# Batch 1's first product: four f tiles dense, eight as seven block products

## The chip, the cores and the metric

The kernel runs on one core of a Trainium2 chip. The metric is the device time of one execution in microseconds. TensorE (PE) multiplies, VectorE (DVE), ScalarE (ACT) and GpSimd (POOL) work on elements, and SyncE (SP) issues the transfers.

## The reference

An attention with two softmaxes gives a token matrix x, and a gated network follows it. Shapes: q, k, v are 8 x 8 x 576 x 64 (batch, head, token, width), p is 8 x 8 x 32 x 64, w_a and w_b are 512 x 1536, w_out is 1536 x 512.

```python
def _attn_ref(q, k, v, p):
    scale = 1.0 / np.sqrt(q.shape[-1])
    def sm_attn(qq, kk, vv):
        s = scale * np.matmul(qq, kk.transpose(0, 1, 3, 2))
        s = s - np.max(s, axis=-1, keepdims=True)
        a = np.exp(s)
        a = a / (np.sum(a, axis=-1, keepdims=True) + 1e-09)
        return np.matmul(a, vv)
    p_packed = sm_attn(p, k, v)
    return sm_attn(q, p_packed, p_packed)
...
x = np.ascontiguousarray(attn_out.transpose(0, 2, 1, 3)).reshape(B * S, H * D)
a = x @ w_a
b = x @ w_b
out = a * b @ w_out
```

## The kernel before, in words

The token matrix is never formed. For each batch the second softmax's weights (256 rows, head and packed token, by 576 tokens, called a2) are kept, and the packed values (ppT) are multiplied with w_a and w_b first: that gives g, 256 rows by 2 x 1536 columns. The first product is then a2 with g, twelve f tiles of 128 columns each for a and b; h is their product; the second product is h with w_out. float32 accuracy comes from splitting each operand in a high and a low part (`_hi`, `_lo`) and three passes: high with high, high with low, low with high. The low part is a subtraction, `lo_part`, on the engine that is named in its call (VectorE, if none is).

**Dense form** (`mm1`, `mm1_half`, L406 to L435; batches 0 and 1). An f tile is 24 matmuls of 288 columns: two halves (a, b) by two halves of the tokens by two row blocks by three passes. The g tiles come from `g_tiles` (L382), with the weights `w_ab` in SBUF, as pairs or single f tiles.

**Block form** (`period`, `product`, L790 to L909; batches 2 to 7). The product of a 2 x 2 block matrix is taken with seven products instead of eight, of sums and differences of the blocks. One f tile is 7 x 3 = 21 matmuls of 288 columns. The sums of the weights come from `make_g` (L801, for two f tiles at once: matmuls, three copies on ScalarE, two sums and a low part on VectorE, a low part and a difference on GpSimd) and `split_g` (G_hi on ScalarE, G_lo on GpSimd, step name "G"); those of a2 from `half_sum` and `half_parts` (steps t0 to t3 and u0 to u3). `split_h` (step "H") makes h_hi on ScalarE and h_lo on GpSimd. Products 1, 5, 3 and 6 go to bank pair X, products 2, 4 and 7 to V; `c` and `d` hold partial sums of them. A period n ends f tile n and begins n + 1: products 5, then 1 and 2 of the next tile; copy X to d on ScalarE; matmuls of the second product as filling; d = V + d on VectorE; products 3, then 6 of the next; c and one multiplication; filling; products 4, then 7 of the next; addition of c and one multiplication; filling. The numbers of filling matmuls stand in `FILLS`.

The weights arrive as float64 words and are converted in batch 0 in three steps, A (high word, ScalarE), B (low word, on the engine that `WAYS` names: 0 ScalarE, 1 VectorE, 2 GpSimd) and C (both joined, VectorE); D splits w_out. `w_ab` is written to DRAM once (`w_kept`, six parts of 1 MB), and `make_g` reads a part for every two f tiles (`load_kept`, tile `wr`).

Every engine works in order. The order is written out by hand: `PLAN_0`, `PLAN` and `STEPS` name the steps between two half f tiles or in the places of a period. `S`, `r` are steps of the first softmax of the next batch, `s` of the second, `k`, `q` transposes of loaded tiles, `L..` loads, `P`, `T` turns of the packed tokens. In batch 1 the dense first product comes first, then a block of 96 matmuls of the second product (`mm2_third`), then two periods (-2 and -1) that begin batch 2's first f tile, then the loop. Three parts of `w_kept` are written after batch 0's second product has been issued in large part, three more at the fourth step of batch 1.

Of the kernel before, what the change touches and what calls it, by code (L numbers as in the profile page):

```python
# [19 lines left out]
def tile_packed_attn_gated_ffn(  # L20
# [20 lines left out]
    nc = tc.nc  # L41
# [14 lines left out]
    NB = 2  # L56
# [15 lines left out]
    scratch = early.__enter__()  # L72
    plain = tc.tile_pool(name="plain", bufs=1, side="right")
# [8 lines left out]
    w_ab = plain_p.tile([P, NC, R, 4 * P], F32, name="w_ab")  # L82
# [39 lines left out]
    def turn(key, b, i):  # L122
# [4 lines left out]
        xTs.setdefault((b, key), []).append(xT)  # L127
# [207 lines left out]
    def stage2(b, e):  # L335
# [43 lines left out]
    ghi = plain_p.tile([P, E, 4, 2 * P], F32R, name="ghi")  # L379
    glo = plain_p.tile([P, E, 4, 2 * P], F32R, name="glo")  # L380

    def g_tiles(b, *groups, s=False):  # L382

        for fts in groups:
# [7 lines left out]
            for r in range(R):  # L392
                for e in range(E):
                    rows = slice(64 * e, 64 * e + 64)
                    w = w_ab[rows, c, r, :].rearrange("p (a u f) -> p u a f", a=2, u=2)
# [23 lines left out]
    def mm1(b, ft, between):  # L419
# [11 lines left out]
        hh = h_hi[ft][:, c0:c0 + S]  # L431
        flat = asb.rearrange("p u t -> p (u t)")
        nc.scalar.copy(out=hh, in_=flat)
        lo_part(h_lo[ft][:, c0:c0 + S], flat, hh, nc.vector if b == 0 and HLO[ft] == "1" else nc.gpsimd)
# [35 lines left out]
    def out_tile(i):  # L470

        if i % 3 == 1:
            return sm.tile([P, DO], F32, name="wo_f32", bufs=1)
# [12 lines left out]
    def emit(b, plan, tasks={}):  # L486

        for name in plan.split():
            if name in tasks:
                next(tasks[name], None)  # L490
                continue
# [30 lines left out]
            elif what == "Lp":  # L522
# [5 lines left out]
    START = ("Y7 k1 X4 k0 T0 k2 k3 k4 q1 B S0 r0 r1 S1 q0 r1 r0 q2 r0 r1 q4 r0 r1 q3 A P0 A X3 Lp2 A s0 s1 s0 "  # L528
             "s1 C Z8 s1 X3 s0 B A B Z9 C B X7 A B C C X5 X15 C s0 A s1 B s0 s1 A B Lk2 B B A s0 B s1 s1 C s0 "
             "s1 g A")  # L530
    WAYS = ("200000020222122211202100021202110111")
    TURN = ("1000100010")
# [3 lines left out]
    PLAN = (" |  |  | S0 | r0 | r0 |  | r0 |  | r0 Lv1 ; S1 | r1 | r1 q0 Lk2 | r1 | r1 | q1 Lk3 Lv2 P0 |  ; s0 | s0 s0 | s0 T2 | "  # L536
            "s0 Lp4 | s0 s1 | s1 s1 | s1 | s1 | s1 | t0 t1 t2 t3 u0 | k2 |  | k3 Lq2")
    PLAN = dict(enumerate(PLAN.split("|")))
    PLAN_0 = ("Lk1 A A B C B C B A C | C B C | A A B | B C A A C A C | | B Lp2 C Lv0 B | | | C k0 T0 B | A A C "
# [447 lines left out]
```

## Time and profile before

| what | value |
|---|---|
| median of 3 runs | 708.11 us (707.4 to 709.52) |
| profiled execution, span from first to last instruction | 705.6 us |
| TensorE busy | 699.4 us (99%) |
| VectorE, ScalarE, GpSimd busy | 455.9, 356.9, 417.1 us |
| instructions | 14386 |

The profiled execution's own time is known by its span; the median of the runs is 2.5 us above it, which holds what lies around the span. A row of a stretch gives the busy time of each engine in it, with the number of instructions in brackets. In the chain a row gives where a piece begins, how long it lasts, and what it is, with the number of instructions; pieces in which TensorE runs one matmul after the other give the spacing of matmuls, while the mean duration of a single matmul holds its way through the array as well. Of a group of instructions the busy time and the mean ns of one are given, then the idle time ahead of them and what ended it.

### The profile page before, as it was taken

To read this page: it belongs to the slowest core of one execution; us is meant where nothing else is said; L and a number is where in the kernel's file an instruction comes from. 1 tells how busy PE (TensorE), PEld (TensorE's weight loads), DVE (VectorE), ACT (ScalarE), POOL (GpSimd) and SP (SyncE) were. 2 spreads that over 40 slices of the span, in tenths; PEclk is the share of its full clock that TensorE was granted. 3 is DMA by queue.
4 is the path that set the end of the run, shared out by engine and by line. 5 is a ranking of instruction groups with operands and counts; after the bars stand their busy time and mean duration, and the time that the engine had idled before them with its cause. 6 is when DMAs were issued, how large, how long until landed. Compare 5 with 4: busy or idle time off the path is not lost.

```text
span 705.6 us, 14386 instructions
## 1 busy us (share of the span) xinstructions
PE 699.4 (99%) x5654; PEld 582.8 (83%) x5654; DVE 455.9 (65%) x833; ACT 356.9 (51%) x719; POOL 417.1 (59%) x321
## 2 busy tenths in 40 slices
PE   9999999999999999999999999999999999999998
PEld 7888878898788888878888788888888878888886
DVE  4997765467365679566775678765785667754332
ACT  3778724554244555535554455554545446544520
POOL 1596741337254777646863589566775578856520
PEclk9999999999999999999999999999999999999999
DMA  9999986753254736356434664556145323133002
GB/s 316 380 229 297 282 233 136 252 106 93 69 141 161 170 89 172 115 139 168 119 95 124 173 161 95 131 165 173 63 123 154 106 91 119 60 124 117 1 1 75
DMA packets 179460, 102.65 MB, mean 145 GB/s; under 512 B 145728, under 2 KB 161344, under 8 KB 174016
## 3 DMA queue, kind: packets, MB, share of 16 engines
q1 hardware_dynamic: 179392, 101.73, 50.7%
q8 instruction: 44, 0.72, 0.4%
q14 instruction: 24, 0.20, 0.1%
HBM read 85.98 MB, written 15.73 MB: 144 GB/s over the span
## 4 chain that ended last, share of the span: by engine, by line
PE 91%; DVE 4%; issue 1%; DMA 1%; ACT 1%; SPq 1%; DVEq 0%
PE x L754 36%; PE m L796 28%; PE m L414 11%; PE m L440 5%; PE x L810 4%; PE s L326 2%; PE s L341 1%; PE x L396 1%; PE s L280 1%; DMA qn<-in_q_dram 1%; PE s L316 1%; DVE a_lo L93 1%; DVE part L764 0%; DVE d L878 0%; DVE w_ab L212 0%
## 5 line engine op out<-in xcount | busy, mean ns | idle before, releaser
L754 PE MATMUL x<-wo,h_hi 128*128 128x512 f32 (+1 forms) x776 | 249.4, 391 | 0.0
L93 POOL TENSOR_TENSOR h_lo<-asb,h_hi 128x576 fp32r<-128x576 f32 x95 | 139.0, 1465 | 76.0 <-ACT h_hi L841 42.8
L754 PEld LDWEIGHTS x<-wo,h_hi 128*128 128x128 f32 x776 | 140.8, 188 | 22.1 <-ACT part L762 0.8
L754 PE MATMUL x<-wo,h_lo 128*128 128x512 f32 (+1 forms) x388 | 152.2, 392 | 0.0
L93 POOL TENSOR_TENSOR G_lo<-gs,G_hi 128x640 fp32r<-128x640 f32 x72 | 113.1, 1577 | 29.6 <-ACT G_hi L831 29.4
L754 PEld LDWEIGHTS x<-wo,h_lo 128*128 128x128 f32 x388 | 72.9, 188 | 11.7
L93 POOL TENSOR_TENSOR A_lo<-gs,A_hi 128x256 fp32r<-128x256 f32 x36 | 27.2, 755 | 89.3 <-ACT A_hi L819 89.3
L878 DVE TENSOR_TENSOR d<-m,d 128x576 f32<-128x576 f32 (+1 forms) x73 | 54.1, 741 | 34.7 <-ACT d L874 33.9
L891 DVE TENSOR_TENSOR asb<-m,d 128x288 f32<-128x288 f32 x72 | 32.5, 451 | 63.2 <-ACT c L887 59.9
L887 ACT COPY c<-m 128x288 f32<-128x288 f32 x72 | 28.8, 400 | 82.5 <-PE m L796 82.5
L764 DVE TENSOR_TENSOR part<-x,part 128x512 f32<-128x512 f32 (+1 forms) x65 | 44.1, 678 | 38.8 <-PE x L754 38.8
L796 PE MATMUL m<-tx_hi,G_hi 128*128 128x288 f32 x216 | 63.8, 296 | 0.0
L796 PE MATMUL m<-tx_hi,G_lo 128*128 128x288 f32 x216 | 63.6, 295 | 0.0
L796 PE MATMUL m<-tx_lo,G_hi 128*128 128x288 f32 x216 | 63.2, 293 | 0.0
L816 ACT COPY gs<-x 128x512 f32<-128x512 f32 x35 | 20.6, 588 | 82.2 <-PE x L810 80.6
L831 ACT CAST G_hi<-gs 128x640 fp32r<-128x640 f32 x72 | 52.2, 729 | 15.7 <-POOL gs L825 15.1
L874 ACT COPY d<-m 128x576 f32<-128x576 f32 (+1 forms) x73 | 46.7, 640 | 19.2 <-PE m L796 18.8
L841 ACT CAST h_hi<-asb 128x576 fp32r<-128x576 f32 x72 | 49.0, 680 | 11.5 <-DVE asb L905 11.5
L796 PEld LDWEIGHTS m<-a_hi,G_hi 128*128 128x128 f32 x144 | 27.0, 187 | 31.9 <-issue 17.4
L825 POOL TENSOR_TENSOR gs<-gs 128x512 f32<-128x512 f32 x36 | 46.7, 1297 | 3.2 <-DVE gs L822 2.9
L796 PE MATMUL m<-a_hi,G_hi 128*128 128x288 f32 x144 | 46.6, 324 | 0.0
L904 DVE TENSOR_TENSOR m<-m,c 128x288 f32<-128x288 f32 x72 | 33.3, 463 | 17.0 <-PE m L796 15.3
(189 smaller groups left out, 1568.9 us busy)
## 6 DMA issues: line engine op xcount, KB each, us to landing
wr<-w_kept SPq DMA_DIRECT2D x36, 1024.0 KB, 5.1
nat<-in_k_dram SPq DMA_DIRECT2D x56, 144.0 KB, 4.7
nat<-in_q_dram SPq DMA_DIRECT2D x56, 144.0 KB, 5.3
vt<-in_v_dram SPq DMA_DIRECT2D x28, 256.0 KB, 3.9
out_dram<-part SPq DMA_DIRECT2D x27, 256.0 KB, 2.1
raw<-in_moe_w_a_dram SPq DMA_DIRECT2D x12, 512.0 KB, 8.7
raw<-in_moe_w_b_dram SPq DMA_DIRECT2D x12, 512.0 KB, 8.7
raw<-in_moe_w_out_dram SPq DMA_DIRECT2D x12, 512.0 KB, 6.9
```

What stands on the lines that cost most here:

```text
L93: return eng.tensor_tensor(out=dst, in0=src, in1=hi.bitcast(F32), op=ALU.subtract)
L414: nc.tensor.matmul(out=ps[:, half, 0:HS], lhsT=gt[:, kt, ft % 4, cols], rhs=at[:, kt, HS * half:HS * half + HS], start=(n == 0 and kt == 0 ...
L440: nc.tensor.matmul(out=o[:, cols], lhsT=ht[:, c0:c0 + P], rhs=wt[:, cols], start=(ft == 0 and n == 0), stop=(ft == NFT - 1 and n == 2))
L754: nc.tensor.matmul(out=o[:, cols], lhsT=ht[:, c0:c0 + P], rhs=wt[:, cols], start=(ft == fts[0] and n == 0), stop=end)
L764: nc.vector.tensor_tensor(out=parts[i][:, cols], in0=o[:, cols], in1=parts[i][:, cols], op=ALU.add)
L796: nc.tensor.matmul(out=bank[:, n % 2, 0:HS], lhsT=g, rhs=t, start=(first and i == 0), stop=(i == 2), skip_group_check=True)
L825: nc.gpsimd.tensor_tensor(out=gs[:, 2:4].rearrange("p a u f -> p a (u f)"), in0=gs[:, 0:2].rearrange("p a u f -> p a (u f)"), in1=s2.unsqu ...
L831: nc.scalar.copy(out=G_hi[:, n % 3], in_=gs[:, 1:6, n % 2])
L841: nc.scalar.copy(out=view(h_hi[ft]), in_=src)
L874: nc.scalar.copy(out=d[:, both], in_=X[:, both, 0:HS])
L878: nc.vector.tensor_tensor(out=d[:, both], in0=V[:, both, 0:HS], in1=d[:, both], op=ALU.add)
L904: nc.vector.tensor_tensor(out=v, in0=v, in1=c2, op=ALU.add)
```

## The change

Batch 1 keeps the dense form for f tiles 0 to 3 and takes the block form for f tiles 4 to 11 (`NB` 1, `F0` 4). Its second product, a block before, now fills the periods 3 to 11, first the first third of all five token tiles (60 matmuls), then the second third of three (36). The two periods ahead of batch 2 and the block of 96 matmuls go. Batch 1's a2 is kept in two layouts: split in full for the dense tiles, then with its differences (steps h0 to h3, j1 to j3) for the block form. Batch 2's attention moves to the steps of batch 1's new plan (`PLAN_1`, `STEPS_1`). Of periods 4 to 11's low parts, five of h and two of G are made by VectorE (`HLO_1`, `GLO`), the others by GpSimd. The six parts of `w_kept` are all written within batch 0 (`K0`, `K1` in the plan, then 5, 4, 3, 2), and the part for f tiles 4 and 5 is loaded ahead of batch 0's last output tile. Tiles take over space of others: `wr` and `gs` that of the weights' parts 0 and 1, `parts` and `d` that of the dense g tiles, `tf` and `A` share one place. `WAYS` and `PLAN_0` get a new order; the plan ahead of batch 0's first product (`START`) stays.

```diff
-    NB = 2
+    NB = 1
+    F0 = 4
...
-    w_ab = plain_p.tile([P, NC, R, 4 * P], F32, name="w_ab")
+    w_ab = [kp.tile([P, R, 4 * P], F32, name=f"w_ab{c}", tag=("wr", "gs")[c]) for c in range(2)]
+    w_ab += [plain_p.tile([P, R, 4 * P], F32, name=f"w_ab{c}") for c in range(2, NC)]
...
-            yield
-            return
-        hi, lo = (t[:, e, :].rearrange("p (x u l) -> p u x l", u=2, l=TL) for t in (a2_hi, a2_lo))
+            if b > NB:
+                yield
+                return
+        rows = "p (u x l) -> p u x l" if halves else "p (x u l) -> p u x l"
+        hi, lo = (t[:, e, :].rearrange(rows, u=2, l=TL) for t in (a2_hi, a2_lo))
...
-    WAYS = ("200000020222122211202100021202110111")
+    WAYS = "200200200222112212222102021211120001"
...
+    for _ in pieces:
+        emit(0, "A B C D")
+    for c in (5, 4, 3, 2):
+        keep_weights(c)
+    for i, c0 in enumerate(tiles):
+        if i == len(tiles) - 1:
+            while slot[0] <= max(PLAN_0):
+                between()
+            g_tiles(1, (0, 1), (2,), s=True)
+            load_kept(F0)
...
-        lo_part(G_lo[:, n % 3], gs[:, 1:6, n % 2], G_hi[:, n % 3], nc.gpsimd)
+        lo_part(G_lo[:, n % 3], gs[:, 1:6, n % 2], G_hi[:, n % 3], nc.vector if GLO[n:n + 1] == "1" else nc.gpsimd)
...
-            lo_part(view(h_lo[ft]), src, view(h_hi[ft]), nc.gpsimd)
+            lo_part(view(h_lo[ft]), src, view(h_hi[ft]), nc.vector if HLO_1[n:n + 1] == "1" else nc.gpsimd)
...
+    GLO, HLO_1 = "010000010100", "010111010101"
+    FIRST_FILLS = ((6, 1, 5), (5, 0, 2), (4, 1, 0), (5, 5, 2), (4, 8, 0), (6, 4, 2), (3, 9, 0), (10, 0, 4), (4, 6, 0))
+    STEPS_1 = {3: {'pre': 'r0', 'a': 'j2 G', 'w': 'r0', 'end': 'S1 Lv1'}, 4: {'pre': 'r1', 'd': 'H', 'v': 'Lk2 r1', 'h': 'q0', 'f': 'r1 r1 G'}, 5: {'d': 'q1 r1', 'a': 'H', 'c': 'P0', 'f': 'G', 'end': 'Lv2'}, 6: {'post': 's0 Lp4 T2', 'v': 's0', 'b': 'G', 'f': 'H s0'}, 7: {'post': 's0', 'a': 'H', 'h': 's0', 'b': 's0 G', 'w': 'Lk3', 'f': 's1'}, 8: {'pre': 's1', 'v': 's1', 'c': 's1 H', 'f': 's0 G'}, 9: {'pre': 'G', 'd': 's1 H k2', 'h': 's1', 'w': 's1 t0', 'end': 't1'}, 10: {'d': 'H', 'v': 'u0 t2', 'a': 'G t3', 'end': 'u1'}, 11: {'v': 'k3', 'a': 'H Lq2', 'w': 'u2 G', 'f': 'u3'}}
+    PLAN_1 = ("h0 h1 h2 j1 h3 | e S0 | j3 | Lq1 M r0 | r0 | | r0 E | Lq0")
...
+    for ft in range(F0):
+        mm1(1, ft, between)
...
+    filler[0] = first_parts()
+    for n in range(F0 - 1, LAST):
```

In `PLAN_1` the name e is the single g group for f tile 3, M is `make_g(4)` and E is `split_g(4)`; h and j are `half_sum` and `half_parts` for batch 1.

## Rows read from the trace of the kernel before

**Rows 1.** The page: span, and busy time of TensorE.

```profile
span 705.6 us, 14386 instructions
...
PE 699.4 (99%) x5654; PEld 582.8 (83%) x5654; DVE 455.9 (65%) x833; ACT 356.9 (51%) x719; POOL 417.1 (59%) x321
```

**Rows 2.** Stretches: PE, PEld, DVE, ACT, POOL busy, granted clock, DMA share, GB/s.

```profile
31.20:80.60 49.40, 49.31 (x469) 42.57 (x469) 41.48 (x67) 38.73 (x71) 38.88 (x24) 1.00 0.97 292
...
118.30:191.90 73.60, 73.60 (x673) 63.16 (x679) 39.08 (x62) 33.43 (x66) 30.48 (x24) 1.00 0.53 135
191.90:358.00 166.10, 166.03 (x1331) 137.33 (x1332) 113.89 (x214) 86.04 (x181) 110.60 (x87) 1.00 0.51 136
```

**Rows 3.** Waits of TensorE: us in total, times, longest.

```profile
PE m L414 <- ACT ghi L402: 0.9, 1, 0.9
```

**Rows 4.** The chain that ended last: start, us, what.

```profile
125.35 0.61 PE m L396 x16
125.96 0.86 PE x L396 x16
...
133.96 3.20 PE m L414 x24
...
167.12 5.46 PE x L754 x24
172.58 1.02 PE m L810 x16
...
193.74 1.40 PE m L796 x9
...
199.52 1.20 PE m L796 x9
```

**Rows 5.** Groups of batch 1's stretch on TensorE, shapes apart.

```profile
L414 PE MATMUL m<-a_hi,ghi 128*128 128x288 f32 x96 | 21.4, 304 | 0.0
```

**Rows 6.** Groups of VectorE, shapes apart: busy us, mean ns, idle before.

```profile
L878 DVE TENSOR_TENSOR d<-m,d 128x576 f32<-128x576 f32 x71 | 53.2, 749 | 30.3 <-ACT d L874 29.5
L764 DVE TENSOR_TENSOR part<-x,part 128x512 f32<-128x512 f32 x63 | 43.2, 686 | 37.0 <-PE x L754 37.0
...
L904 DVE TENSOR_TENSOR m<-m,c 128x288 f32<-128x288 f32 x72 | 33.3, 463 | 17.0 <-PE m L796 15.3
L905 DVE TENSOR_TENSOR asb<-m,d 128x288 f32<-128x288 f32 x72 | 33.0, 458 | 2.5
L891 DVE TENSOR_TENSOR asb<-m,d 128x288 f32<-128x288 f32 x72 | 32.5, 451 | 63.2 <-ACT c L887 59.9 <-POOL G_lo L93 1.4 <-POOL h_lo L93 0.7
L93 DVE TENSOR_TENSOR a_lo<-t,a_hi 128x288 fp32r<-128x288 f32 x24 | 20.1, 857 | 0.6 <-ACT a_hi L646 0.6
...
L821 DVE TENSOR_TENSOR gs<-x,gs 128x256 f32<-128x256 f32 x35 | 14.8, 424 | 22.9 <-ACT A_hi L818 21.3 <-ACT A_hi L819 1.4
...
L93 DVE TENSOR_TENSOR A_lo<-x,A_hi 128x256 fp32r<-128x256 f32 x35 | 14.6, 418 | 0.0
...
L93 DVE TENSOR_TENSOR tx_lo<-tf,tx_hi 128x576 fp32r<-128x576 f32 x6 | 11.9, 1983 | 1.1 <-POOL h_lo L93 1.1
...
L286 DVE TENSOR_REDUCE nmx<-s 128x1 f32<-128x576 f32 x15 | 11.2, 749 | 0.4 <-PE s L280 0.4
```

**Rows 7.** Groups of GpSimd, shapes apart.

```profile
L93 POOL TENSOR_TENSOR h_lo<-asb,h_hi 128x576 fp32r<-128x576 f32 x95 | 139.0, 1465 | 76.0 <-ACT h_hi L841 42.8 <-ACT h_hi L433 32.3
L93 POOL TENSOR_TENSOR G_lo<-gs,G_hi 128x640 fp32r<-128x640 f32 x72 | 113.1, 1577 | 29.6 <-ACT G_hi L831 29.4
```

**Rows 8.** Line 93 alone: duration ns min/median/max, first and last start.

```profile
L93 DVE TENSOR_TENSOR h_lo<-asb,h_hi x1: 759/759/759, 69.0 to 69.0; 128x576 fp32r<-128x576 f32 x1
```

**Rows 9.** Transfers by line: count, KB each, median us to landing.

```profile
wr<-w_kept SPq DMA_DIRECT2D x36, 1024.0 KB, 5.1
...
w_kept<-w_ab SPq DMA_DIRECT2D x6, 1024.0 KB, 7.1
```

**Rows 10.** SP in order of time, 80 to 120 us.

```profile
97.54 2.24 SPq L626 DMA_DIRECT2D w_kept<-w_ab  x3
...
116.00 1.77 SPq L467 DMA_DIRECT2D out_dram<-asb  x4
```

More of the change, by code (lines that the diff above doesn't have):

```diff
@@ L430, in mm1 @@
         c0 = 64 * (b % 2)
[L431 to L434, printed above, removed]
+        hh, hl, src = h_hi[ft][:, c0:c0 + S], h_lo[ft][:, c0:c0 + S], asb.rearrange("p u t -> p (u t)")
+        if b:
+            hh, hl = (t.rearrange("p (x u l) -> p u x l", u=2, l=TL) for t in (hh, hl))
+            src = asb.rearrange("p u (x l) -> p u x l", l=TL)
+        nc.scalar.copy(out=hh, in_=src)
+        lo_part(hl, src, hh, nc.vector if b == 0 and HLO[ft] == "1" else nc.gpsimd)
         between()
@@ new lines, in tile_packed_attn_gated_ffn, with between, load_kept @@
+    slot = [0]
+    def between():
+        emit_steps(1, PLAN_0.get(slot[0], ""))
+        slot[0] += 1
+    for ft in range(NFT):
+        if ft % 2 and ft + 1 < NFT:
+            g_tiles(0, (ft + 1, ft + 2))
+        mm1(0, ft, between)
+    LAST = NFT * (B - NB)
+    wr_of, A_of, parts = {}, [], []
+    def load_kept(n):
+        if n < LAST:
+            t = kp.tile([P, R, 4 * P], F32, name="wr", tag="wr")
+            nc.sync.dma_start(out=t.rearrange("p r f -> p (r f)"), in_=w_kept[n // 2 % NC])
+            wr_of[n] = t
@@ new lines, in tile_packed_attn_gated_ffn @@
+    tiles = tiles_of(0)
+    pairs = [bank_pair() for _ in range(2)]
+    banks = [pairs[i % 2][:, i // 2, :] for i in range(4)]
+    for f in range(9):
+        for i, c0 in enumerate(tiles):
+            mm2_part(banks[i], c0, [f])
+        between()
[3 more added lines that the diff above has]
+        keep_weights(c)
+    for i, c0 in enumerate(tiles):
+        if i == len(tiles) - 1:
+            while slot[0] <= max(PLAN_0):
+                between()
+            g_tiles(1, (0, 1), (2,), s=True)
+            load_kept(F0)
+        for f in range(9, NFT, 3):
+            mm2_part(banks[i], c0, range(f, f + 3))
+            between()
+        mm2_out(0, banks[i], c0, i)
@@ L747, in flush, with mm2_steps @@
             pend.pop(0)()
-    def mm2_steps(o, c0, fts, then, cols=slice(0, DO)):
+    def mm2_steps(o, c0, fts, then, cols=slice(0, DO), first=True, last=True):
         for ft in fts:
@@ L754, in mm2_steps @@
                 nc.tensor.matmul(
-                    out=o[:, cols], lhsT=ht[:, c0:c0 + P], rhs=wt[:, cols], start=(ft == fts[0] and n == 0), stop=end)
-                if end:
+                    out=o[:, cols], lhsT=ht[:, c0:c0 + P], rhs=wt[:, cols],
+                    start=(first and ft == fts[0] and n == 0), stop=(last and end))
+                if end and then:
                     pend.append(then)
@@ L872, in period @@
         if here or there:
[L873 removed]
+            d = d_of[n] = late["d"][:, n % 2]
             nc.scalar.copy(out=d[:, both], in_=X[:, both, 0:HS])
@@ new lines, in tile_packed_attn_gated_ffn @@
+    for ft in range(F0):
+        mm1(1, ft, between)
+    while slot[0] <= max(PLAN_1):
+        between()
+    t = kp.tile([P, 4, DO], F32, name="parts", tag="ghi")
+    parts += [t[:, i] for i in range(4)] + [late["part"]]
+    t = kp.tile([P, 4 * DO], F32, name="tf_d", tag="glo")
+    late["tf"] = t[:, 0:3 * HS].rearrange("p (i c) -> p i c", i=3)
+    late["d"] = t[:, 3 * HS:7 * HS].rearrange("p (i u c) -> p i u c", i=2, u=2)
+    banks_of["x"], banks_of["v"] = bank_pair(), bank_pair()
+    paired[0] = True
```

176 lines of the change are left out of this document (61 added, 115 removed), and 4 rows, old and new, of the table PLAN_0.

## The prediction

> **What bounds the kernel now.** I read the page's first part, then the stretches, then TensorE's waits, then the chain that ended last. TensorE is busy for 699.4 of 705.6 us [rows 1]. A busy TensorE is not yet one at its peak, so the stretches come next: in batch 0's first product (31 to 81 us), in batch 1's stretch (118.3 to 191.9 us) and in two batches' worth of the loop (191.9 to 358 us) TensorE is busy nearly throughout at the full granted clock, while VectorE, ScalarE and GpSimd are each busy for less [rows 2]. After the start TensorE's own row of waits has one entry, 0.9 us [rows 3]. The chain stays on TensorE, and its spacing can be read there: 24 dense matmuls of 288 columns take 3.20 us, nine block matmuls of the same width 1.20 us, both 0.133 us each; 24 matmuls of 512 columns take 5.46 us, 0.2275 us each [rows 4]. So TensorE runs at its own rate. Time falls by what its list of matmuls loses and rises by any wait that comes in.
>
> **The change part by part.**
>
> *The products.* A dense f tile is 24 matmuls; batch 1's 288 are three groups of 96, of which one row is shown [rows 5]. The change leaves 4 x 24 dense ones and makes 8 tiles of seven products with three passes each, 8 x 21 = 168. Removed: 192 x 0.133 = 25.6 us. Added: 168 x 0.133 = 22.4 us. Difference: -3.2 us.
>
> *Forming g.* Removed are two of the three single groups (0.61 us each) and three pairs (0.86 us each): 3.8 us. Added are four block formings at n = 4, 6, 8 and 10, at the 1.02 us of the one at 172.58 us: 4.1 us [rows 4]. Difference: +0.3 us. The single group for f tile 3 and the forming for batch 2 stay.
>
> *Second product.* The first third of batch 1 (5 tiles) and three tiles of the second third are 8 x 12 = 96 matmuls of 512 columns in both kernels; they now stand between the block products. Difference: 0.
>
> *Going to and fro.* After a group of narrow matmuls the first wide ones are late: nine block matmuls behind a forming take 1.40 us, elsewhere 1.20 [rows 4], so 0.2 us a change. Batch 1's stretch has some nine such places and the new one, with its formings apart from the attention groups, one or two more; bounds 0 and +0.5, taken as +0.1.
>
> TensorE's list therefore gets shorter by 2.8 us. Whether anything stands idle for it is the rest.
>
> *VectorE in the new stretch.* Batch 1's stretch of 73.6 us [rows 2] less 288 x 0.133, 96 x 0.2275, three singles and three pairs, one forming and the twelve block matmuls ahead of batch 2 leaves 6.3 us for attention and changes. From f tile 4 on the new stretch holds nine periods: 180 matmuls at 0.133 (24.0), 96 at 0.2275 (21.8), four formings (4.1) and nearly all of those 6.3 us, say 5.8: 55.7 us of TensorE. VectorE's work I take from the loop: 113.89 us for two batches [rows 2], 57 us per batch of twelve periods. The new stretch lacks four of twelve periods' own operations (0.749 + 0.451 + 0.463 + 0.458 = 2.12 us each, 8.5), two of six formings (0.424 twice and 0.418, 2.5), six of nine additions to parts (0.686 each, 4.1) and half of the first softmax, by estimate two operations of 0.749, 1.5 [rows 6]. That leaves 40.4, and 41.3 with one more split at 0.857 [rows 6]. To it come the differences that now go to VectorE instead of GpSimd: five of h and two of G. The one h difference that VectorE made in this trace took 0.759 us [rows 8]; by size (640 instead of 576 elements) one of G is 0.84. The seven cost 5.5 us. But the same subtraction at the same size, tx_lo, averages 1.983 us [rows 6]; at this price the seven cost 5 x 1.98 + 2 x 2.2 = 14.3. So VectorE has 46.8 to 55.6 us to do in 55.7 us, 84 to 100%, where the loop stands at 69% [rows 2]. On average it fits at either end.
>
> A queue that is so full answers late. Behind a late difference on VectorE stand the addition into d (0.749), the two multiplications for h and the addition of c; the third and fourth product, and the next period's second product, wait for the banks that these read. In the written order an even period ends with 2 to 4 matmuls of the second product and an odd one is followed by a forming, so that about 0.5 to 1 us of lateness is covered; without that cover each lateness is TensorE's. The worst places are period 5 (a transpose of q ahead of the addition into d, and only five filling matmuls), period 9 (a softmax transpose, which waits for GpSimd's multiplication, ahead of the addition of c) and periods 10 and 11 (the splits of batch 2's transposed weights). Bounds: 0, and 7 x (1.983 - 0.759) = 8.6 us if every one of the seven is slow and all of it reaches TensorE. I take +0.4, near the lower end, because GpSimd loses the same seven operations (five of 1.465, two of 1.577 us [rows 7]) and with them work that VectorE could collide with.
>
> The tx_lo row against the h row shows a VectorE subtraction that takes 2.6 times as long in one place as in another. The Trainium skill ("SBUF — State Buffer", section "SBUF: two separate sides") states that a VectorE instruction with two SBUF inputs and a GpSimd instruction exclude one another from a shared port pair, and that whoever starts second is blocked for the other's whole length. The two rows agree with it so far. By that rule most of the seven would stand near tx_lo's figure, and the sum would be the third case below.
>
> *Writing and reading w_kept.* The same six writes of 1 MB, but parts 0 and 1 go out within the second product of batch 0 and 5, 4, 3, 2 behind them. A write takes 7.1 us to land [rows 9]; the three of before are issued from 97.54 us [rows 10], 20 us ahead of batch 1, so four have time even at twice that. SP then passes the stores of three output tiles, the last of which ends at 117.8 us [rows 10], and issues the load of part 2 there; it lands 5.1 us later [rows 9], near 123. The first forming stands behind four half tiles (6.4 us), the group for f tile 3 (0.6) and a scores group (0.6), near 126 us. Cover of 3 us; at the 7.1 us of a write 1 us of it is left, and without it the forming and all that TensorE has behind it wait, by 1 or 2 us at most. I take 0. Later loads have two periods, some 12 us, for their 5.1.
>
> *New places in SBUF.* tf, x5, d, parts, gs and A take over space of weights, g tiles and an output tile. Their first writers wait for the last readers: GpSimd's half sums for the writes of parts 4 and 5, which are out first; the first d and parts for dense f tile 3, which TensorE has then just finished. V's bank waits for VectorE's product of tile 3 (0.75 us and a hand-over), behind three matmuls (0.4 us) and the transposes of a softmax that the step ahead issues. Bounds 0 and 0.5; it is within the 0.4 above.
>
> *Batch 0's new order.* Of the 36 low-word conversions GpSimd now makes 16 instead of 13, ScalarE 11 instead of 13, VectorE 9 instead of 10. GpSimd is busy 38.9 of 49.4 us there [rows 2] and can take more, but the h differences behind come later, and with them the buffer that ScalarE's next copy needs. TensorE's list is unchanged, so that little can be won. Bounds -0.3 and +1.5; taken as 0.
>
> Sum: 705.6 - 3.2 + 0.3 + 0.1 + 0.4 = 703.2 us of span. The median of the runs is 708.11, 2.5 us above the span of the profiled execution, and I leave that as it is: **705.7 us**.
>
> **The rivals.**
> (1) *The gain comes, as above.* TensorE's list is surely shorter, and the loop runs the same block products at their full rate beside a busy VectorE. 704.3 to 706.0. Chance 0.51.
> (2) *VectorE's queue eats it.* TensorE waits some 0.35 us at each of the seven, about 2.5 us: 708.1 - 2.8 + 2.5 = 707.8. A late load (1 to 2 us) or GpSimd's conversions (up to 1.5) lead to the same case. For it: 84 to 100% against 69. Against: the loop too has periods that take the splits of the transposed weights, and no wait of TensorE shows there [rows 3]. 706.0 to 710.2. Chance 0.34.
> (3) *Slower, by one mechanism:* the seven differences each get tx_lo's 1.983 us, ahead of what TensorE wants, and the lateness can't be made up, since VectorE idles in other places of the period. Of the 8.6 us two thirds reach TensorE, 5.7: 708.1 - 2.8 + 5.7 = 711.0. It decides from 4.9 us on. For it: the tx_lo row. Against: less GpSimd work to collide with. 710.2 to 713. Chance 0.15.
>
> **How the numbers follow.** 0.3% (2.1 us) is about what a measurement of this kernel can't tell from no change: faster is below 706.0, slower above 710.2. Faster 0.51, same 0.34, slower 0.15. The low end of the range is the whole list with nothing lost and the small change of batch 0 won, with about half a microsecond of spread, 704.3; the high end cuts into the third case, 709.9. The likeliest case's own range is 704.3 to 706.0.
>
> **What the next profile would show.** Dense matmuls: 384 instead of 576; block matmuls 1680 instead of 1512. From batch 1's first matmul to the first step of batch 2's own periods: 70.8 to 71.5 us instead of 73.6, at 0.133 us a matmul, with no gap over 0.4 us. Wrong, if the h differences on VectorE average over 1.5 us and the gaps behind the addition into d add up to over 1 us; if the load of part 2 lands behind 126 us; if batch 1 starts later than 118.6 us; or if two batches of the loop behind it no longer take the time they took.

## The result and the profile after

The changed kernel takes 712.26 us (median of five runs, 711.95 to 712.98) where the kernel before took 708.09 beside it: a ratio of 1.0053, interval 1.0041 to 1.0066. It is about 4 us slower; 2.4 us less had been forecast. In every run of this case the time lies 1.73 to 1.86 us above the span. So the profile of the kernel before, of 705.6 us, belongs to a run of 707.4, the quickest of its five; of the 2.5 us between that span and the median 0.7 come from this, and only 1.8 lie around the span. The profile below is of a run of 712.11. The two spans differ by 4.7 us, the medians by 4.2.

The page of the changed kernel first, span and busy times, as [rows 1]:

```profile
span 710.3 us, 14408 instructions
...
PE 701.7 (99%) x5614; PEld 580.3 (82%) x5614; DVE 472.1 (66%) x870; ACT 365.8 (51%) x742; POOL 439.6 (62%) x337
```

TensorE is busy 2.3 us longer although its list of matmuls got shorter, which says that a busy TensorE can be a slow one. So the stretches come next, as [rows 2]: batch 0's first product, 73.6 us from batch 1's start, and two batches of the loop.

```profile
32.60:84.00 51.40, 50.77 (x467) 42.71 (x468) 43.62 (x70) 37.28 (x68) 44.02 (x26) 1.00 0.95 278
121.61:195.21 73.60, 72.61 (x623) 59.60 (x622) 51.24 (x96) 41.45 (x89) 41.50 (x35) 1.00 0.61 150
197.20:363.30 166.10, 166.03 (x1340) 137.62 (x1332) 115.72 (x221) 86.81 (x183) 110.99 (x87) 1.00 0.51 136
```

The first product of batch 0 now lasts from 32.56 to 84.03 us: 2 us longer. In batch 1's stretch TensorE is idle for 1 us, and VectorE works 51 us where it worked 39.

The same matmul can be looked up in both traces, and where the distance between the two grows, time is lost:

| this matmul begins at, us | before | after | later by |
|---|---|---|---|
| batch 0, f tile 0, the first dense one | 31.16 | 32.56 | 1.40 |
| batch 0, f tile 5 | 51.74 | 54.15 | 2.41 |
| batch 0, f tile 8 | 63.97 | 67.37 | 3.40 |
| batch 0, second product | 80.60 | 84.03 | 3.43 |
| batch 1, first | 118.15 | 121.61 | 3.46 |
| product 5, the first of batch 2's own periods | 193.67 | 197.21 | 3.54 |
| 60 f tiles (of 21 block matmuls) behind batch 2's first block matmul | 603.02 | 607.26 | 4.24 |
| 63 f tiles behind it | 621.79 | 626.66 | 4.87 |

Three losses stand there: 3.4 us before batch 0's second product, nothing gained where the list got shorter (batch 1's stretch takes 75.6 us in both by this measure), and 1.3 us in a loop whose instructions are the same. (Below, as in the expectations, an f tile of the block form and its period go by one running number, and "product 9" can be f tile 9.)

TensorE's waits of the changed kernel, as [rows 3]:

```profile
PE m L419 <- ACT ghi L407: 1.4, 1, 1.4
...
PE m L775 <- DVE asb L877: 0.5, 1, 0.5
PE m L775 <- DVE tf_d L864: 0.4, 1, 0.4
...
PE m L419 <- ACT asb L431: 0.3, 1, 0.3
PE m L775 <- DVE a_lo L96: 0.2, 1, 0.2
```

The 1.4 us (0.9 before) is the wait for the first g tile, ahead of the first dense matmul. The 0.3 is in batch 0, the 0.5 and 0.4 stand in period 10 of batch 1, the 0.2 at 612 us in the loop. Each of the last three has a VectorE instruction at its end, and the chain through period 10 (start, us, what) shows which was slow:

```profile
185.30 1.84 DVE h_lo L96
187.13 0.67 DVE tf_d L864
187.80 0.06 DVE a_lo L96
187.86 0.23 issue
188.09 1.82 DVE a_lo L96
189.91 0.38 DVE asb L877
...
190.33 1.53 PE m L775 x9
```

Beside it VectorE and GpSimd in order of time, same kernel (start, us, engine, line, what):

```profile
185.22 1.30 POOL L810 TENSOR_TENSOR gs<-gs 128x512 f32<-128x512 f32 x1
186.47 1.32 POOL L624 TENSOR_TENSOR tf_d<-t,t 128x288 f32<-128x288 f32 x1
187.76 1.84 POOL L96 TENSOR_TENSOR G_lo<-gs,G_hi 128x640 fp32r<-128x640 f32 x1
...
185.30 1.84 DVE L96 TENSOR_TENSOR h_lo<-asb,h_hi 128x576 fp32r<-128x576 f32 x1 [0.21 <-ACT h_hi L827]
187.06 0.75 DVE L864 TENSOR_TENSOR tf_d<-m,tf_d 128x576 f32<-128x576 f32 x1
187.72 2.19 DVE L96 TENSOR_TENSOR a_lo<-t,a_hi 128x288 fp32r<-128x288 f32 x2
```

The h difference that took 0.759 us alone [rows 8] takes 1.84 here: it began 0.08 us behind GpSimd's difference for gs. With it the addition into d is late, and product 4 of the period and then product 5 of the next begin late, by 0.57 and 0.66 us from start to start; TensorE's row of waits has 0.4 and 0.5 for them, since it counts from the end of the matmul before.

**TensorE's account of batch 1's stretch** (first dense matmul to product 5 of batch 2's own periods), from start to start of neighbouring matmuls, against steady spacings of 0.1325 us (dense and block matmuls, 288 columns) and 0.229 us (second product, 512 columns). A spacing more than 0.03 us above these counts as late. Narrow matmuls are those of attention and of the formings of g.

| us | before | after |
|---|---|---|
| late spacings at the edges of narrow groups | 16, costing 1.53 | 20, costing 1.92 |
| other late spacings: waits, and the matmul behind a wait | none | 16, costing 2.66 |
| narrow matmuls (forming, attention) | 12.06 | 12.11 |
| spread over single matmuls | 0.20 | 0.34 |
| length | 75.52 | 75.59 |

The 24 matmuls saved are 3.2 us; 0.39 went into four more edges at 0.1 us each, 2.66 into waits, and 0.2 into the rest. Six of the 16 other late spacings, 0.64 us together, stand directly behind a wait: the matmul after the one that waited is 0.10 to 0.11 us late as well. (The expectations further on count these six among the changes, as 26 changes, and give the waits without them, 1.9 us.)

The fillings are not in this bill. From 288 to 512 columns or back TensorE goes 37 times in the changed kernel's stretch and 7 times in the other's; outside waits that costs 0.08 and 0.02 us, as part of the spread. Both kinds of change can be seen in one piece of the loop of the kernel before:

```profile
330.89 1.06 PE L810 MATMUL x<-wr,ppT 64*32 64x512 f32 x16
331.89 0.40 PE L796 MATMUL m<-a_hi,G_hi 128*128 128x288 f32 x1
332.12 0.30 PE L796 MATMUL m<-a_lo,G_hi 128*128 128x288 f32 x1
332.26 0.29 PE L796 MATMUL m<-a_hi,G_lo 128*128 128x288 f32 x1
...
333.06 0.29 PE L796 MATMUL m<-a_hi,A_lo 128*128 128x288 f32 x1
333.19 0.63 PE L754 MATMUL x<-wo,h_hi 128*128 128x512 f32 x2
...
333.89 0.40 PE L754 MATMUL x<-wo,h_hi 128*128 128x512 f32 x1
334.12 0.30 PE L796 MATMUL m<-a_hi,G_hi 128*128 128x288 f32 x1
334.25 0.30 PE L796 MATMUL m<-a_lo,G_hi 128*128 128x288 f32 x1
```

Behind the forming the second block matmul begins 0.23 us after the first, 0.10 more than the steady spacing. Into the filling (0.13 us) and out of it (0.23, then 0.13) the spacings are the steady ones.

### The profile page after: what moved, and what is told of

It reads as the page before. It is cut to its first block, busy times and chain, and to the rows that moved or that the text cites. A ratio compares the mean times of both kernels' runs of the same rounds, so it can differ in the third digit from the quotient of the medians.

```text
span 710.3 us, 14408 instructions
## 1 busy us (share of the span) xinstructions
PE 701.7 (99%) x5614; PEld 580.3 (82%) x5614; DVE 472.1 (66%) x870; ACT 365.8 (51%) x742; POOL 439.6 (62%) x337
## 4 chain that ended last, share of the span: by engine, by line
PE 81%; DVE 7%; DMA 6%; ACT 3%; issue 2%; SPq 0%; DVEq 0%; ACTq 0%
PE x L732 36%; PE m L775 30%; PE m L447 5%; PE x L789 5%; DMA raw<-in_moe_w_a_dram 2%; PE s L329 2%; DVE a_lo L96 1%; PE s L344 1%; PE m L419 1%; DMA vt<-in_v_dram 1%; DVE w_ab L215 1%; DMA raw<-in_moe_w_b_dram 1%; DVE asb L434 1%; PE s L319 1%; PE s L283 1%
## 5 line engine op out<-in xcount | busy, mean ns | idle before, releaser
L96 POOL TENSOR_TENSOR G_lo<-gs,G_hi 128x640 fp32r<-128x640 f32 x78 | 122.9, 1581 | 27.4 <-ACT G_hi L817 26.1
L96 POOL TENSOR_TENSOR A<-gs,A 128x256 fp32r<-128x256 f32 x40 | 30.9, 773 | 95.9 <-ACT A L804 95.9
L864 DVE TENSOR_TENSOR tf_d<-m,tf_d 128x576 f32<-128x576 f32 (+1 forms) x81 | 60.0, 741 | 33.3 <-ACT tf_d L860 32.6
L877 DVE TENSOR_TENSOR asb<-m,tf_d 128x288 f32<-128x288 f32 x80 | 36.0, 449 | 66.6 <-ACT c L873 63.4
L775 PE MATMUL m<-a_hi,A 128*128 128x288 f32 x320 | 77.3, 298 | 0.2
L775 PE MATMUL m<-tx_hi,G_lo 128*128 128x288 f32 x240 | 70.9, 296 | 0.0
L775 PE MATMUL m<-tx_lo,G_hi 128*128 128x288 f32 x240 | 70.8, 296 | 0.0
L860 ACT COPY tf_d<-m 128x576 f32<-128x576 f32 (+1 forms) x81 | 51.8, 640 | 21.4 <-PE m L775 21.0
L775 PEld LDWEIGHTS m<-a_hi,A 128*128 128x128 f32 x320 | 55.9, 188 | 1.3 <-DVE asb L891 0.9
L743 DVE TENSOR_TENSOR parts<-x,parts 128x512 f32<-128x512 f32 x56 | 38.4, 685 | 22.7 <-PE x L732 22.6
```

Of the source, the lines that this page charges most:

```text
L96: return eng.tensor_tensor(out=dst, in0=src, in1=hi.bitcast(F32), op=ALU.subtract)
L743: nc.vector.tensor_tensor(out=parts[i][:, cols], in0=o[:, cols], in1=parts[i][:, cols], op=ALU.add)
L775: nc.tensor.matmul(out=bank[:, n % 2, 0:HS], lhsT=g, rhs=t, start=(first and i == 0), stop=(i == 2), skip_group_check=True)
L860: nc.scalar.copy(out=d[:, both], in_=X[:, both, 0:HS])
L864: nc.vector.tensor_tensor(out=d[:, both], in0=V[:, both, 0:HS], in1=d[:, both], op=ALU.add)
L877: nc.vector.tensor_tensor(out=hf[:, 1], in0=X[:, k0, 0:HS], in1=d[:, k0], op=ALU.mult)
```

## The experiments

### Batch 0: the list of words and the order of steps

**b0_new_order.** The kernel before with batch 0's new lists; the products stay as they were.

```diff
-    WAYS = ("200000020222122211202100021202110111")
+    WAYS = "200200200222112212222102021211120001"
```

and PLAN_0 as the change has it, without K0 and K1, the two loads of q in its last slot.

> The kernel before with the new WAYS and PLAN_0 alone (without the two writes in the plan, and with the two loads of batch 2's q at its end as before). Theory A, the new order of batch 0 delays TensorE by some 2 us there and some 0.4 us at the start: about 710.5 us, and batch 0's second product begins 2 to 2.5 us later than in the kernel before. Theory B, the delay in batch 0 came with the new places in SBUF and the early writes: 708.1 us, and the second product begins where it did.

710.2 us, ratio 1.0032 (1.002 to 1.0044): 2.3 us of loss without any of the products changed. In its trace the first dense matmul begins 0.78 us later than before, batch 0's second product 2.66 later, and from there to the end the distance stays at 2.65.

**old_order.** The other way about: the changed kernel with the old lists.

```diff
-    WAYS = "200200200222112212222102021211120001"
+    WAYS = "200000020222122211202100021202110111"
```

and PLAN_0 as before, with K0 and K1 in its slots 28 and 33.

> The changed kernel with the old WAYS and the old PLAN_0 (the two early writes of weights put into it). Theory A: some 2.4 us less than the changed kernel, 709.8 us, and the second product of batch 0 begins within 1 us of where it began in the kernel before. Theory B: no change, 712.3 us.

709.49 us, 1.0019 (1.001 to 1.0028). Against 1.0053 that gives back 2.4 us, as much as b0_new_order lost: theory A holds in both. Only the place of batch 0's second product missed its forecast: it begins at 81.86 us, 1.26 later than in the first profile of the kernel before and 0.19 later than in its second (before_again).

**new_ways_only** and **new_steps_only** take b0_new_order apart: the first line above alone, and PLAN_0 alone.

> Kernel: the kernel before with the new list of where each word of the weights is formed, and nothing else. Theory (the list makes the start later, three profiles with it have the first dense matmul at 31.94 to 32.56 us, six without it at 31.06 to 31.48; the order of steps makes the rest): first dense matmul at 31.9 to 32.6, from there to the second product as before (49.4 us, or 50.4 where the weights of f tile 5 land late), time 0.8 to 1.3 us over before. Rival (the list only matters together with the new order): 0 to 0.4 us.

709.21 us, 1.0019 (1.0008 to 1.003).

> Kernel: the kernel before with the new order of batch 0's steps and the old list of where each word is formed. Theory as in new_ways_only: first dense matmul at 31.0 to 31.5 us, from there to the second product 51.3 us where before has 49.4, time 1.0 to 2.0 us over before. Rival (order and list fit each other, and mixing them costs more): 2 to 4 us over before.

711.24 us, 1.0037 (1.0025 to 1.0049). Alone they cost 1.3 and 2.6 us, which is more than the 2.3 of both at once, so they can't be added; the 2.6 lies in the rival's range, by which mixing them costs more. What belongs to the list of words is the first wait. TensorE's waits of new_ways_only, then those of new_steps_only:

```profile
PE m L414 <- ACT ghi L402: 1.4, 1, 1.4
PE m L414 <- DVE asb L429: 0.6, 1, 0.6
```

```profile
PE m L414 <- ACT ghi L402: 0.9, 1, 0.9
PE m L414 <- ACT asb L426: 0.4, 1, 0.4
```

**old_first_ways.** The changed kernel with the first ten entries of the list as before.

```diff
-    WAYS = "200200200222112212222102021211120001"
+    WAYS = "200000020222112212222102021211120001"
```

> The changed kernel with the engines of the first ten low-word conversions as in the kernel before. Theory A, the fourth conversion on GpSimd blocks VectorE's joining of words at the start: the first dense matmul comes 0.4 to 0.5 us earlier, 711.8 us. Rival: the start is late by its transfers alone, and it comes where it did, 712.3 us.

711.42 us, 1.0048 (1.0034 to 1.0062): within the error of the changed kernel's time. Its first dense matmul is back at 31.09 us, so the rival (transfers alone) is out for the start; from there to the second product it loses 2.04 us as the changed kernel does (2.03).

All profiles together part the two. The five with the new first ten entries of the list have their first dense matmul at 31.8 to 32.6 us, the twelve without at 31.0 to 31.6. From there to the second product the six with the new order of steps take 51.3 to 52.3 us, with either list, and the eleven with the old order 49.4 to 50.4.

How a word formed on GpSimd costs TensorE time can be read at f tile 7. In the changed kernel, with the chain's row below:

```profile
61.33 3.10 DVE L215 SCALAR_TENSOR_TENSOR w_ab<-raw 128x512 uint32<-128x512 uint32 x3
62.33 2.33 POOL L209 TENSOR_SCALAR raw<-raw 128x512 uint32<-128x512 uint32 x1
64.36 0.74 DVE L434 TENSOR_TENSOR asb<-m,asb 128x576 f32<-128x576 f32 x1
...
65.15 0.30 PEld L419 LDWEIGHTS m<-a_hi,ghi 128*128 128x128 f32 x2 [0.41 <-DVE asb L434]
```

```profile
62.71 1.72 DVE w_ab L215 x2
```

The kernel before at the same multiplication:

```profile
58.77 1.64 DVE L212 SCALAR_TENSOR_TENSOR w_ab<-raw 128x512 uint32<-128x512 uint32 x2
```

Three joins of words take 3.10 us where two took 1.64 in the kernel before, and the multiplication that frees TensorE's bank stands behind them. Of VectorE's 36 joins nine take over 1 us in the changed kernel, five in the kernel before. That these joins make all of batch 0's loss is argued, not shown.

### Batch 1: who makes the differences, and where they stand

**all_lo_gpsimd.** The changed kernel with the seven differences of the new periods back on GpSimd.

```diff
-    GLO, HLO_1 = "010000010100", "010111010101"
+    GLO, HLO_1 = "000000000000", "000000000000"
```

> The changed kernel with all h and G differences of batch 1's block tiles on GpSimd. Theory A, VectorE's queue costs TensorE its waits in periods 10 and 11 through the one h difference of period 10: 1.2 to 2 us less, 710.5 us, and no gap of over 0.3 us behind it. Rival: GpSimd, with seven operations of 1.5 us more in some 55 us, becomes late with h and G itself and the time stays or rises, 712 to 714 us.

711.59 us, 1.0048 (1.0034 to 1.0062), within the error of the changed kernel's time. The two waits of period 10 are gone, but four others of 0.14 to 0.50 us have come; the late spacings outside the edges cost 2.94 us, the stretch takes 76.2. Theory A's gain of 1.2 to 2 us did not come. Which of the two engines has the work made no difference that these four runs can tell.

**no_h_lo.** old_order without eight ninths of the h differences of f tiles 4 to 10, so it leaves out part of h's low words.

```diff
-            lo_part(view(h_lo[ft]), src, view(h_hi[ft]), nc.vector if HLO_1[n:n + 1] == "1" else nc.gpsimd)
+            k = slice(S // 2 // TL - 32 // TL, S // 2 // TL) if n < NFT - 1 else slice(0, S // 2 // TL)
+            lo_part(view(h_lo[ft])[:, :, k], src[:, :, k], view(h_hi[ft])[:, :, k],
+                    nc.vector if HLO_1[n:n + 1] == "1" else nc.gpsimd)
```

> Kernel: old_order without eight ninths of the h_lo differences of products 4 to 10 of the second batch (four on VectorE, three on GpSimd; the last ninth stays), so it leaves out part of the low words of h. It prices the work that the block products added to VectorE and GpSimd. Theory V (those differences and the port they share are the 1.9 us of waits): waits fall to 0.3 to 0.7 us, the stretch from 75.5 to 74.0 to 74.3, the time about 1.3 us under old_order's. Rival (the waits stem from the order of the other steps, the t and u steps of the next batch, and from ACT): waits stay at 1.5 or more.

708.57 us, 1.0004 (0.9995 to 1.0013). The stretch takes 75.39 us (75.50 in old_order), with 2.44 us of waits and matmuls behind them (2.52; without those matmuls, as the expectation counts, 1.77 and 1.91), where theory V had 0.3 to 0.7 and 74.0 to 74.3: as an account of the waits it falls. The time is 1.1 us under old_order's, close to V's 1.3, but the two intervals overlap, and of the 1.3 us between the spans of the two profiles 1.0 lies in batch 0's first product (49.42 and 50.38 us), which the edit leaves alone. Only the wait for d went; the next, 0.65 us, stayed. VectorE and GpSimd of this kernel at that place show why:

```profile
182.16 1.30 POOL L810 TENSOR_TENSOR gs<-gs 128x512 f32<-128x512 f32 x1
...
182.23 1.31 DVE L96 TENSOR_TENSOR h_lo<-asb,h_hi 128x64 fp32r<-128x64 f32 x1 [0.20 <-ACT h_hi L827]
183.46 0.75 DVE L866 TENSOR_TENSOR tf_d<-m,tf_d 128x576 f32<-128x576 f32 x1
184.12 2.19 DVE L96 TENSOR_TENSOR a_lo<-t,a_hi 128x288 fp32r<-128x288 f32 x2
```

A difference of 64 columns takes 1.31 us, as long as GpSimd's instruction ahead of it needs to end. Here it isn't the amount of work that makes VectorE late but that it stands in line behind GpSimd. The Trainium skill ("SBUF — State Buffer", section "SBUF: two separate sides") states that VectorE with two SBUF inputs and GpSimd share a pair of ports as an exclusive lock, and that whoever comes second is blocked until the first is done; these rows agree.

**h9_later** and **h9_end**, both on old_order, move that one difference, with ScalarE's copy ahead of it, behind the first half of h of the period, and behind both. Of the line `STEPS_1` the entry that changes is shown.

```diff
-10: {'d': 'H', 'v': 'u0 t2', 'a': 'G t3', 'end': 'u1'}
+10: {'v': 'u0 t2', 'a': 'G t3', 'c': 'H', 'end': 'u1'}
```

> Kernel: the changed kernel with the old order of batch 0 (as old_order, 709.5 us), and h_lo of product 9 moved in period 10 behind the product that needs hf1, so that VectorE forms d first. Theory V (the two waits of period 10, 0.57 and 0.65 us in old_order, come from a VectorE h_lo of 1.84 us that stands in front of the d add while GpSimd holds the SBUF port): the 0.57 us wait goes, the 0.65 us wait shrinks to under 0.3, the stretch falls from 75.5 to 74.4 to 74.7 and the time to 708.3 to 708.8. Rival G (GpSimd's queue, full from 183.8 to 190.6 us, is what is late, and VectorE only shows it): the waits come back at the next instruction in line, the a_lo pair, and the time stays at 709.2 to 709.8.

709.73 us, 1.0013 (1.0005 to 1.0022). Both waits went, but the forecast of theory V (708.3 to 708.8) did not come: a product now began 1.0 us late (0.8 in TensorE's row of waits), for the second half of h, which now stood behind the difference:

```profile
PE m L775 <- DVE asb L891: 0.8, 1, 0.8
```

```diff
-10: {'d': 'H', 'v': 'u0 t2', 'a': 'G t3', 'end': 'u1'}
+10: {'v': 'u0 t2', 'a': 'G t3', 'end': 'H u1'}
```

> Kernel: old_order with h_lo of product 9 moved in period 10 to its end, behind both halves of h of product 10. In the trace of h9_later the wait had moved to product 3 of product 11 (1.0 us, for the DVE half of h that stood behind h_lo, 1.39 us). Theory V2 (what counts is only what stands ahead of the two halves of h on VectorE): that wait falls under 0.3, waits in the stretch from 1.82 to about 1.0, the stretch from 75.3 to 74.4, the time 0.8 us under h9_later's: about +0.1 against before. Rival G (VectorE and GpSimd together are full in periods 10 and 11): the wait comes back in period 11, the stretch stays over 75.1 and the time at +0.7 to +1.2 us.

708.03 us, 0.9996 (0.9986 to 1.0005): even with the kernel before, 1.6 us under old_order and, with the old order of batch 0, 4 us under the changed kernel. No wait over 0.1 us of periods 9 to 11 is left in its trace, where old_order has 1.5 us more. Theory V2 holds for these waits and for the time. The stretch of its profile (75.24 us) came out longer than expected, only 0.26 us under old_order's, since late spacings of 0.31, 0.50 and 0.24 us stood in its dense part; the profiled run (709.27) is also one of the slower of its eleven. What makes the dense part's waits stays open.

**two_fills.** old_order with the filling matmuls (512 columns) of six of the nine periods in fewer stretches.

```diff
-FIRST_FILLS = ((6, 1, 5), (5, 0, 2), (4, 1, 0), (5, 5, 2), (4, 8, 0), (6, 4, 2), (3, 9, 0), (10, 0, 4), (4, 6, 0))
+FIRST_FILLS = ((6, 6, 0), (5, 2, 0), (5, 0, 0), (6, 6, 0), (4, 8, 0), (6, 6, 0), (3, 9, 0), (10, 4, 0), (4, 6, 0))
```

> Kernel: old_order with the fillings of the seven new periods in fewer stretches (6,1,5 to 6,6,0 and so on; the same number of filling matmuls in all but product 4's and 5's periods, within one or two). Theory C (a change of kind costs about 0.1 us each, whatever stands around it): changes in the stretch fall from 26 to 18 and their cost from 2.54 to 1.75 us, so 0.8 us less if waits stay at 1.9: 708.7 us. Rival W (the fillings cover the waits): the changes fall as said, but the waits grow by 0.5 to 1.5 us where the third stretch of filling was, and the time is 709.2 to 710.2.

713.15 us, 1.0054 (1.004 to 1.0068), over both forecasts. In its profile, which is of the slowest of its five runs (715.54), waits with the matmuls behind them grow to 7.2 us (the longest 1.5) and the stretch to 81.3. Most of it are waits for the two halves of h (TensorE's waits):

```profile
PE m L775 <- DVE asb L891: 1.9, 3, 1.3
PE m L775 <- DVE asb L877: 1.1, 1, 1.1
```

Theory C falls: 18 spacings at the edges of narrow groups cost 1.92 us, as 20 cost 1.93 in old_order, for the edit moves fillings, not attention or formings; and the fillings' own changes, 33 instead of 37, cost 0.07 us instead of 0.10. There was nothing to win. Rival W holds in kind, since the stretches of filling that were taken away had covered waits, but the waits grew by 4.7 us and not by 0.5 to 1.5.

**h9_end_M.** h9_end with the first forming for the block products one slot earlier.

```diff
-    PLAN_1 = ("h0 h1 h2 j1 h3 | e S0 | j3 | Lq1 M r0 | r0 | | r0 E | Lq0")
+    PLAN_1 = ("h0 h1 h2 j1 h3 | e S0 | j3 M | Lq1 r0 | r0 | | r0 E | Lq0")
```

> Kernel: h9_end with the first forming of g for the block products one slot earlier in the second batch's dense part (behind the sixth slot's steps instead of the seventh's), so that ACT's three copies for it do not stand ahead of the copy of f tile 2's product. Theory A (the waits of 0.44 to 0.50 and 0.24 us in f tiles 2 and 3 are that ACT queue): both go, the stretch falls from 75.2 to 74.5, the time 0.5 to 0.7 us under h9_end's, 0 to 0.6 us under before's. Rival (the copies come in the way of f tile 1's product instead, or the weights are not there yet): the wait moves, no gain, -0.2 to +0.4 us against before.

708.97 us, 1.0004 (0.9995 to 1.0013): no gain. The load of part 2 lands too late for it (order of time, TensorE):

```profile
126.12 1.09 PE L789 MATMUL x<-wr,ppT 64*32 64x512 f32 x16 [1.42 <-DMA wr<-w_kept]
```

The rival holds. In the changed kernel that load is issued at 121.6 us and lands 5.8 us later, 2 us ahead of the forming at 129.37.

### The loop

**race_fix_before.** The kernel before with the split of g behind the differences of A in every second batch's period 11 (an entry of `STEPS`).

```diff
-11: {'post': 'u1', 'v': 'H', 'a': 'k3', 'h': 'Lq2', 'c': 'u2 G', 'f': 'u3'}
+11: {'post': 'u1', 'v': 'H', 'a': 'k3', 'h': 'Lq2', 'c': 'u2', 'f': 'u3 G'}
```

> Kernel: the kernel before with one step moved, in the period of product 11 of every second batch: the split of g (an ACT copy and a GpSimd difference) behind the last differences of A instead of ahead of them. Theory P (GpSimd's G_lo and VectorE's a_lo start within 20 ns of each other there, and whichever starts second is held until the first is done; lost at 273.7 and 439.9 us, won at 605.8 us, worth about 0.6 us each): the long a_lo (1.65 us) go, the time falls by 0.6 to 1.3 us to 706.8 to 707.5. Rival Q (PE has slack there, the loss is swallowed): no change, 707.8 to 708.4. If G_lo is then late for its product, slower: 708.5 to 709.5.

708.27 us, 0.9999 (0.999 to 1.0007). The place is the one at 607 us in the table. The kernel before there, then the changed one:

```profile
605.79 0.45 DVE L93 TENSOR_TENSOR a_lo<-t,a_hi 128x288 fp32r<-128x288 f32 x1
...
605.81 1.85 POOL L93 TENSOR_TENSOR G_lo<-gs,G_hi 128x640 fp32r<-128x640 f32 x1
```

```profile
610.01 1.54 POOL L96 TENSOR_TENSOR G_lo<-gs,G_hi 128x640 fp32r<-128x640 f32 x1
...
610.02 1.85 DVE L96 TENSOR_TENSOR a_lo<-t,a_hi 128x288 fp32r<-128x288 f32 x1
```

20 ns ahead, VectorE's difference takes 0.45 us; 10 ns behind, 1.85. In the edited kernel the long ones at 273.7 and 439.9 us are short (0.43 us), but the second difference of each pair now begins behind GpSimd's and takes 1.48 us. TensorE is 0.45 and 0.44 us earlier there, the next period takes all of it back, and at 607 us it loses 0.70. At each of these three places TensorE's row of waits names ScalarE's copy for g (0.2, 0.2 and 0.6 us), which the late split delays. Rival Q holds.

**reordered_before.** The kernel before with three tiles reserved behind tx; no instruction differs.

```diff
-    A_hi = lp.tile([P, E, 4, P], F32R, name="A_hi")
-    A_lo = lp.tile([P, E, 4, P], F32R, name="A_lo")
-    gs = lp.tile([P, 6, 2, P], F32, name="gs")
...
     late["tx_lo"] = lp.tile([P, 3, HS], F32R, name="tx_lo")
+    A_hi = lp.tile([P, E, 4, P], F32R, name="A_hi")
+    A_lo = lp.tile([P, E, 4, P], F32R, name="A_lo")
+    gs = lp.tile([P, 6, 2, P], F32, name="gs")
```

> Kernel: the kernel before with the tiles A and gs reserved behind tx instead of ahead of it, so that tx_hi, tx_lo and tf lie elsewhere in SBUF; no instruction differs. Theory L (the loop of the changed kernel runs 0.5 to 0.6 us longer over products 14 to 58 because its operands lie elsewhere, 1 to 3 ns a matmul): spacing from product to product shifts by 1 to 3 ns here too, the loop changes by 0.2 to 0.6 us either way. Rival (the loop's drift belongs to something else that the change does, and addresses do not matter): every spacing within 0.2 ns of before's, the loop the same within 0.05 us.

706.85 us (median of 10), 0.998 (0.9971 to 0.9989): faster than both kernels. From f tile 14 to f tile 58 of the loop it takes 305.68 us. The six other profiles with the old places have 306.07 to 306.16, the ten with the changed kernel's places 306.68 to 306.79. Single spacings moved by nanoseconds: wide matmul to wide matmul with h_hi 230.5 to 228.9 ns (164 of them), a_lo's to a_hi's 133.2 to 131.7 (85). In the changed kernel it is other pairs: tx_lo's matmul to the one behind it 130.7 to 133.8 (123 of them, 0.38 us). Theory L holds for this kernel: where the tiles lie sets some ns a matmul. That the changed kernel's 0.5 us in the loop have the same cause fits its shifted spacings, but no run put its tiles back, so that is argued, not shown.

### What repeats

**before_again** and **after_again** are the two kernels unedited.

> The kernel before, once more, for its profile alone. If the start varies from run to run: the first dense matmul lies between 30.9 and 31.9 us (31.16 in the first profile) and the first copy of kT between 5.5 and 6.1. If the later start of the changed kernel (32.56) is its own, this one lies within 0.1 us of 31.16. The span then 705.3 to 706.5.

709.07 us, span 707.3. The first dense matmul begins at 31.31 us, near the 31.16 of the first profile. But f tile 5 then begins 1.09 us later than there: the forming ahead of it took 2.16 us instead of 1.55. Forming groups of that length, and a step of 0.6 to 0.9 us with them, are also in old_order, two_fills and h9_end, and not in race_fix_before and h9_later; and the 607 us place is lost here by 0.67. So both are steps that the kernel before takes in one run and not in another.

> The changed kernel once more, for its profile. If the shift of the start and of batch 0 belongs to the kernel: first dense matmul 31.8 to 32.6 us, 2.0 us more than before's from there to the second product, waits of 0.57 and 0.65 us in period 10 again. If they varied from run to run, at least one of the three is gone.

711.25 us, span 709.5. First dense matmul at 32.12 us, 51.33 us from there to the second product (51.47 in the first profile; the kernel before has 49.44 and 50.36), and the two waits of period 10 at 0.58 and 0.65 us: these losses are the kernel's own. Batch 0's between those two points is 1.0 to 2.0 us, by the profile of before that one takes.

## Why the prediction was wrong

The prediction's sum for the span was -3.2 +0.3 +0.1 +0.4 and nothing for batch 0 and the loop. By its own steps, of which two failed by some 2.3 us each, batch 0's new order and the waits:

- *The products*: right. 384 dense and 1680 block matmuls, at the spacings named. *Second product*: right, it cost nothing.
- *Forming g*, +0.3: right, the formings take 0.2 us more in the stretch; attention takes 0.2 less, so that narrow matmuls as a whole take 0.05 more.
- *Going to and fro*, +0.1 with a bound of +0.5: 0.4, within the bound. Its price held: 0.2 us for a narrow group are two late spacings, one at either edge, of 0.1. Its number nearly held: 16 edges became 20, two groups more. At its own price one or two more groups are 0.2 to 0.4, not 0.1.
- *VectorE in the new stretch*, +0.4: 2.7 us of waits with the matmuls behind them, within its bounds but not for its reason. The load of VectorE was not it: VectorE was busy for 45.0 of 57.8 us from f tile 4 on, 78% where 84 to 100 had been forecast; six of the seven differences took 0.75 to 0.82 us and one 1.84; and without most of the h differences 2.4 us remained (no_h_lo). What cost 1.4 of the 2.7 was one instruction's place: in line behind a GpSimd instruction and ahead of the addition into d and of both halves of h (h9_end takes it away). The prediction named periods 10 and 11 among the worst and the port as the way; it took GpSimd's lighter queue as a reason against, yet GpSimd was busy without a gap over 0.2 us from 183.8 to 190.6 us there. Of the rest 0.8 us stand between 133 and 139 us, in f tiles 2 and 3 and right behind them, and 0.4 in small pieces; no run shows their cause.
- *Batch 0's new order*, taken as 0 with +1.5 as its bound: wrong, and beyond its bound. It costs 2.3 us by b0_new_order and 2.4 by old_order. The prediction compared GpSimd's busy share (79% of that stretch) and stopped there. By the rows at f tile 7 VectorE's joins stand beside GpSimd's words, and the bank's release stands behind the joins; that this is the whole of it is argued, not shown.
- *Writing and reading w_kept*, 0: right, though the load lands at 127.4 us, not near 123, since SP's queue and batch 1 both came later. The prediction had named a landing behind 126 and a start of batch 1 behind 118.6 as signs of being wrong; the first came at no cost, the second (121.61) was batch 0's loss.
- *The loop*, taken as unchanged: its instructions are, its operands' places aren't. 0.5 us from f tile 14 to f tile 58, with the places as the likely cause, and at 607 us a step of 0.6 us that falls either way.

With what was measured: -3.2 + 0.05 + 0.4 + 2.7 + 0.15 for the stretch, + 2.3 for batch 0, + 0.7 for the loop's drift up to 607 us and -0.2 for what lies behind: 2.9 us. The ratio says 3.8 and the medians 4.2. The step at 607 us is lost in all ten profiles with the new products and won in two of the six without them (race_fix_before, which edits that place, left out); it can be at most 0.6 of the rest, and by these counts is some 0.2. Whether it falls that way by the change, and what list and order of batch 0 are each worth in the time, stays open, and so does the remainder.

The third rival's range (710.2 to 713) holds the measured time, but by luck: its mechanism, every difference at 1.98 us, is not what happened, since the h differences on VectorE average 0.94 us over the whole kernel.

## What to carry to other kernels

A lower count of matmuls is worth what remains after the waits that the new order brings: of 3.2 us saved here 2.7 went into waits and the matmuls behind them and 0.4 into more edges of narrow groups, while thirty more changes between 288 and 512 columns cost less than 0.1. Measure the price of each kind of change in the trace before counting them. Where VectorE and GpSimd both work from SBUF, ask of each VectorE instruction that TensorE waits for what stands ahead of it and what GpSimd has just begun; moving one instruction gave 1.6 us of time here and took 1.5 us of waits away, while cutting seven to a ninth left 2.4 of 2.5 us of waits. Changes that ride along (an order of steps, a list of engines, a place in memory) are priced alone, or they hide what the main one gave.

## What was not expected of the hardware

- Where tiles lie in SBUF changes the spacing of the same matmuls by 1 to 3 ns, 0.5 us over 306 us, and the time of reordered_before by 0.2%, of which the loop explains a part and the rest is open. (By the order of three tiles alone that is shown for the kernel before; for the changed kernel's 0.5 us the other way it is argued.)
- A VectorE instruction that reads two operands from SBUF can take four times as long for having begun 10 ns behind GpSimd's instead of 20 ns ahead (1.85 us against 0.45), whatever its own size: 64 columns took 1.31 us.
- GpSimd's conversion of words (some 2 us) does not hold VectorE to its end: in the two first profiles the 20 joins that began 0.5 us or more behind the start of such a conversion took 0.67 to 0.70 us beside it, and the 13 that began sooner behind it 0.77 to 1.18. The rule cited above from the Trainium skill ("SBUF — State Buffer", section "SBUF: two separate sides") would have both wait for its end; the measurement decides. For GpSimd's differences of two operands the rows above agree with that rule.
